# A new order for the operations of a fused gated-delta-rule and softplus-FFN kernel, from the 88th operation on

## The chip, the cores and the metric

The kernel runs on one NeuronCore of a Trainium2 chip. The metric is the device time of one execution in microseconds (us), input and output in the chip's main memory. Five engines work side by side, each through its own list in order: PE (matrix products), DVE and ACT (vector and activation work), POOL (vector work, and issue of some transfers) and SP (issue of transfers). They wait for one another by semaphores.

## The reference, cut to what matters

For each of 4 batches and 8 heads a 48 x 48 state is carried over 768 positions; the result goes through a feed-forward layer.

```python
k_n = k / (norm(k, axis=-1) + 1e-6)
for t in range(768):
    readout = q[t] @ state
    y[t] = g[t] * readout
    v_old = state.T @ k_n[t]
    state = state + beta[t] * outer(k_n[t], v[t] - v_old)
x = y as (3072 tokens, 384)
out = softplus(x @ w_in) @ w_out          # 384 -> 2048 -> 384
```

Inputs and output are float32; the kernel computes products in float16 with float32 accumulation.

## The kernel before, in words

The 768 positions are cut into 12 chunks of 64. Within a chunk the recurrence is turned into matrix products, for which each chunk needs the inverse of a 64 x 64 triangular matrix per head; only the state passes from chunk to chunk. Chunks 2i and 2i+1 share one inverse, so there are six inverses, named here by their first chunk (0, 2, 4, 6, 8, 10).

The function `load` (and `load_q`, for q) moves a chunk's k, q, v, g in two halves each, nearly all by SP; buffers are few (kf 3, qf 2, vf 3, gf 3), so a load often waits until an operation on DVE, ACT or POOL has freed one. The weights w_in (w0.0 to w0.3) and w_out (w1.0 to w1.3) are eight transfers that POOL issues.

The steps of a chunk pair, with the names used below:

- norms (`norms`): `ksq` (ACT, square, line 545), `red` (DVE, sum, 549), then the square root: `sqrt` on ACT for chunks 0 to 3, `pow` on POOL (566) for the others, and `eps` (DVE, 570 and 572). `kmul` (327) multiplies k by the result.
- products of k and q (`front`): `cast` of q to float16, transposes `trs` (345 for k, 388 for q), their copies `kev`, the products `gram` (503, and 432 and 461 for the first pair), from which `kkc` copies and `mask` (518) multiplies.
- the inverse (`inverse`): `kd0`, `kd1` (604) and `ln` (611) lay out the diagonal blocks; `clear` (619), `diag` (621) and `prep` (629) set up; 15 `step`s (639 and 646) eliminate, row by row, each needing the one before. For pair 0 this is on DVE, for all others on POOL. `cv` (228) and `c16` turn the result to float16, `tn` (667) and `t32` (686) transpose it on DVE, and PE completes the inverse by `xmm` (707), `tmm` (732) and `zmm` (770), with `xs`, `tlo`, `thi`, `z` between them.
- the chain from chunk to chunk (`chain`): `vs` and `w0` (first pair), `ks` and `qs` (813), `w` (847), `umm` (855), `u1`, `zu` (878), `u2`, `smm` (898), `s` (the new state, 913), `ymm` (928), `y` (943), `ytr` (962), `xt`.
- the feed-forward layer (`dense`): 96 groups `g1` (992), each followed by `soft` on ACT (1004), and 96 groups `g2` (1019), then a copy `o` and two stores per 128 tokens. `h`, into which g1 writes, has two buffers.
- 24 `warm` groups on PE (1064) that multiply the identity and whose result nobody reads.

Each step is an operation with a number (0 to 1255). What sets the order is a table written out in the program, `_ORDER` (line 1074 on): each word is an engine's letter (P = PE, D = DVE, A = ACT, G = POOL, S = SP) and an operation's number. `emit` goes through it, asserts that all that an operation depends on has been emitted, gives it its buffers in the order of the table, and puts its instructions at the end of that engine's list. So the table sets each engine's order, the engine of those operations that several engines can do, and which operation gets which buffer. Nothing is reordered later.

Of the kernel before, what the change touches and what calls it, by code (L numbers as in the profile page):

```python
# [1071 lines left out]


_ORDER = """
S0 D158 P1232 P1234 P1233 P1235 A1 P1236 P1238 D111 P1237 P1239 P114 A9 A104 D105 A110 P112 S8
A106 D115 P1241 D113 P124 P121 A123 D134 P137 A138 D133 P135 P1243 D125 P147 D107 D122 A136 P144
A108 P1240 P127 P1242 A149 P1249 A148 A146 D126 P1248 D109 D156 S19 S18 A145 S2 P1250 A206 P207
S3 A116 A117 A208 P118 A120 S5 S17 A119 P150 A152 S12 A129 S33 A154 D159 S27 S26 D157 D160 D161
D162 D163 D164 D165 D166 D167 D168 D169 D170 D171 P128 S16 D172 D173 D174 P1251 D175 D176 D177
P1244 A197 S25 D198 A222 P223 A224 G179 S11 A140 D178 G238 G239 P1245 A131 P1246 P1247 S24 A199  # L1080
P181 D180 S10 A139 P184 A182 D200 S4 D588 D132 D130 G188 A185 G187 P183 A190 P193 D194 A189 A594
P595 S13 A589 S32 P590 A201 D202 D203 D219 P186 A596 A591 P597 A598 P592 P605 A593 P603 S7 S6
D606 D604 A191 P204 P609 P607 A587 S34 D192 A275 D205 P209 D608 P214 S35 S42 S43 D211 A610 D210
D216 P220 G96 A212 A217 A215 D213 P141 A221 A142 A143 D218 D276 S41 S40 A277 P600 P599 D601 D602
P195 G300 D196 P872 D278 G99 A873 P230 A231 P225 A228 P1255 A226 A233 A235 D232 D229 D227 D611
D234 P874 A875 P886 D236 P619 P612 D620 D613 P151 D155 A284 P884 G98 A887 A885 G97 S14 D237 P285
P1254 A286 P882 P301 A883 A302 P615 A616 S49 P622 A623 P876 S15 A877 P878 G100 G101 G103 P614
P617 G279 D280 P621 P624 D153 S48 A879 A625 A618 G102 D281 P282 D297 P1252 D283 P630 D631 P632
D633 P292 A293 P298 A299 P880 A881 P634 A295 G240 G241 D294 D635 G242 G243 G244 G245 G246 P1253
G247 G248 P303 A304 G249 G250 G251 G252 G253 D306 D307 S50 P308 D296 A309 A311 P904 A905 P916  # L1090
A917 D312 P287 A290 D288 A313 P914 G254 G255 G256 D305 A915 P888 P910 A911 D314 D315 P627 P626
D629 D628 A353 D257 D258 P912 A913 P908 D354 P889 G259 D260 A909 G316 G317 P906 A907 G318 G319
G320 P902 A903 P890 P891 S57 A892 S56 P261 A262 G321 A267 P264 D265 A355 P895 P896 D291 P638
P266 P263 A270 D289 P643 P636 D310 G322 P897 P898 A268 P271 D356 G357 S20 S21 D644 A269 A899
P646 A647 D637 P639 A640 P918 S51 D362 P363 D272 A364 P641 A642 P645 P648 A649 S59 S58 A378 D358
P919 P920 P921 A922 D359 P650 P651 D653 P654 D652 S22 S23 D655 P656 P273 P925 P379 D657 A380
D274 P660 P667 P658 G323 G324 G325 G326 G327 A659 P926 P669 S28 S29 D668 G375 P670 A671 S65 S64
A431 D661 P663 D664 P927 D432 P672 A673 P662 P665 A666 S31 P360 D361 P376 S30 P678 D679 A377
P680 D681 P365 A366 D367 A368 D369 P928 P682 D683 P381 D383 A384 G328 G329 G330 G331 G332 G333
P386 A389 D388 D387 P956 S72 S73 A433 D385 A957 D434 P962 P370 D371 D390 D372 A963 A373 A382  # L1100
P954 A955 P936 A937 A391 P675 S74 P674 P934 G334 A935 G335 D336 S66 D374 S67 G440 G337 D676 S894
S36 D338 D677 D392 P944 S901 A945 S923 P342 A343 D393 P339 P952 A953 S37 S44 A340 A346 P948 A949
P441 P940 A941 A345 P684 P691 D692 D685 A442 P341 P693 P344 D348 G435 D436 A347 D453 P942 A943
S75 P932 A933 P349 P687 P694 S81 S80 P686 G394 S45 D350 A509 G395 G396 G397 G456 G398 P960 G399
S924 S39 A695 A961 A929 P950 D688 P689 D690 P454 S38 A951 P946 A947 P938 S88 A939 P457 G400 A458
G401 G402 G403 G404 G405 D510 P958 A959 S89 P964 G406 G407 S893 S931 S91 P702 D703 S930 S90 P351
S54 P696 D697 D352 A511 D512 P965 P966 P967 D968 S970 G408 G409 G410 P698 A455 P459 A462 D461
D463 P699 D460 D700 P971 P972 D701 P973 P974 P464 D437 S900 P704 A975 S85 S969 P708 A465 P438
D468 A467 D466 D709 D705 P978 P715 D716 P711 A439 A712 P979 P448 D450 D452 D451 D449 P718 S47
S46 S60 G534 G411 S53 G412 A415 A719 D416 P710 P713 A714 P980 P981 P443 D445 D447 P717 P720 A982  # L1110
S52 A444 P726 D727 P985 A721 P706 A446 A469 P728 A424 D729 P722 P723 P535 A536 P730 D707 P986
P987 D731 P1000 S55 G513 A1001 P1014 A1015 D470 S83 D471 A423 P988 A989 P1008 P1010 G413 A1009
D414 P420 A1011 P417 A418 D724 D514 D725 D531 P1018 A1019 P994 A995 A421 P532 D533 D515 P998
A999 P739 P732 D733 S82 A518 P734 P419 P422 D740 G472 G473 G474 G475 D426 P1004 A1005 D425 P996
A997 P429 P427 P742 D430 A743 P735 A736 P1002 D428 A1003 P519 P741 P744 P737 G476 A745 P1020
A1021 D738 S991 S70 D520 G477 S983 P516 P1006 P750 D751 S977 A517 A1007 S69 S976 P542 D544 D545
A543 D546 P752 P992 S71 A993 D753 P1016 A1017 P521 D523 A522 D525 P746 A524 P747 S990 D748 D749
P1022 A1023 P1012 G478 G479 G480 A1013 G481 P526 D530 A527 A529 P537 A540 D539 D538 P763 D541
P1024 P1025 P754 S984 P1026 P1027 D528 P756 P758 S84 A755 S61 D764 P766 S87 A1028 G482 G483 G484
G485 G486 G487 G488 G489 G490 G491 D492 P495 S63 P498 S62 D757 S1030 A767 A499 A496 G547 P759  # L1120
D548 D549 P1031 P1032 P1033 P1034 A1035 S1037 P765 D760 G493 D494 A501 A502 P768 D769 P761 D762
P1038 P1039 P776 D777 P771 P774 P497 P500 S76 A503 P770 D775 P778 D779 P1040 P1041 A1042 P1070
A1071 P1062 A1063 P1045 P1072 A1073 S68 S1036 P1058 A1059 P1046 P1054 A1055 P1074 D772 D773 P780
D781 P787 P1047 A1075 P1048 A1049 P1064 A1065 S77 S1043 P1060 A1061 P783 A784 D788 P790 A791
G550 G551 G552 G553 G554 G555 G556 G557 G558 G559 G560 G561 G562 G563 G564 D504 P505 P1056 S78
A1057 P1080 A1081 P782 D506 P785 D786 G565 G566 G567 G568 G569 G571 P789 P792 D793 P1052 A1053
P1066 A1067 P798 D799 P794 P795 D796 P1078 A1079 D797 P1082 P804 D805 A1083 P813 P811 D812 S79
P507 P807 D572 D508 A580 D570 S1050 S1044 S93 D808 P800 D801 S1029 P814 D815 P1068 A1069 P1076
A1077 P1084 P1085 P1086 P1087 D1088 P816 A817 P806 P809 D810 S95 P576 P573 A574 S1051 P824 D825
P802 A803 S1089 P1091 P1092 P1093 P1094 P818 P822 D823 A577 P578 A1095 S1097 P575 A581 P819 D582  # L1130
D820 P826 A827 S1090 P1098 P1099 P1100 P1101 A1102 S86 S94 S1103 P1132 A1133 P1114 A1115 P1105
P1126 A1127 D821 P828 P837 D829 P835 P583 P1138 A1139 P1116 A1117 P1106 P1107 P1120 A1121 P1108
A1109 S1111 S92 P1140 A1141 D836 D584 D579 P838 A839 P831 A832 P1134 A1135 P1128 A1129 P840 A841
P830 P833 P1112 A1113 S1104 S1110 P848 D834 P846 P843 P842 P1118 A1119 P1130 A1131 D844 D845
P852 P859 P1122 D847 A1123 D849 P850 D851 D860 D853 P1124 A1125 P1142 A1143 P1144 P1136 P1145
P1146 A1137 P1184 A1185 P1147 D1148 S1149 S1150 P1178 P862 D863 P855 D856 P585 D586 A1179 P1158
P1159 P1160 P1161 A1162 P854 P857 A858 P861 P864 P1151 P1152 P1153 P1154 D1155 S1156 S1157 P1172
D865 P1174 P1165 P1166 A1173 A1175 P1167 P1168 D1169 S1170 S1096 P1182 A1183 P1176 A1177 P868
D869 P866 D867 P1186 A1187 P1180 A1181 P870 S1171 P1188 P1189 D871 P1204 A1205 P1208 A1209 P1190
P1191 A1192 S1194 P1206 A1207 S1193 P1212 A1213 P1195 P1196 P1202 P1210 A1203 A1211 P1197 P1198  # L1140
D1199 S1200 S1201 P1216 A1217 P1214 S1163 P1218 P1219 P1220 A1215 P1221 A1222 S1223 S1164 S1224
P1225 P1226 P1227 P1228 A1229 S1231 S1230
"""

# [1 line left out]
_INS = ['q', 'k', 'v', 'beta', 'g', 'moe_w_in', 'moe_w_out']  # L1146
_OUTS = [((3072, 384), 'float32')]


# [23 lines left out]
```

## Time and profile before

| | |
|---|---|
| median of 3 runs | 257.73 us (255.1 to 258.18) |
| the profiled execution, its own time | 255.46 us |
| its span, first to last instruction | 253.6 us |
| PE busy | 236.9 us (93%), 5040 matmuls |
| DVE, ACT, POOL busy | 153.7, 153.0, 127.1 us |
| moved by DMA | 27.56 MB |

Times in the profile count from the start of the span. "Busy" is the time in which an engine had an instruction in execution; matmuls overlap, so a busy PE need not be at its peak. "L707" is line 707 of the program. In a timeline a row gives start, duration, engine, line, operation, what is written and read, the number of instructions, and in brackets how long the engine had been idle before it and who ended that. PEclk is the clock that was granted to PE, in tenths of full speed.

### The profile page before, as it was taken

What the parts mean: (1) busy time and instruction counts of PE and PEld (TensorE: products, weight loads), DVE (VectorE), ACT (ScalarE), POOL (GpSimd) and SP (SyncE); (2) the same over time, 40 slices, a digit from 0 to 9 for tenths busy, and PEclk for the clock granted to TensorE, in tenths of its full rate; (3) what the DMA queues carried; (4) which work ended last, traced back from release to release, by engine and by line L of the source; (5) the groups of instructions that cost most, each with busy time, mean ns of one, the idle gap of its engine ahead of it and who ended that gap; (6) DMA issues with size and microseconds to landing.
All of it is one profiled execution on the core that took longest, in us unless ns stands there. A gap on an engine that the chain in (4) does not pass through costs nothing.

```text
span 253.6 us, 11355 instructions
## 1 busy us (share of the span) xinstructions
PE 236.9 (93%) x5040; PEld 160.5 (63%) x5040; DVE 153.7 (61%) x311; ACT 153.0 (60%) x285; POOL 127.1 (50%) x227
## 2 busy tenths in 40 slices
PE   7976588998989999999999999999999999999993
PEld 3543577676766765666766767755676565777751
DVE  7789888775893699759697588523843315313000
ACT  3557777686866579973777675456453475223530
POOL 8201653978879889988948859884000000000000
PEclk9999757799999999999999999999999999999999
DMA  8999999999990789083943850643024130112113
GB/s 111 198 181 178 178 179 180 186 195 176 176 153 6 173 180 157 4 200 83 156 98 84 170 99 22 124 83 80 3 66 93 23 80 0 34 32 48 34 47 78
DMA packets 86192, 27.56 MB, mean 109 GB/s; under 512 B 76288, under 2 KB 86144, under 8 KB 86144
## 3 DMA queue, kind: packets, MB, share of 16 engines
q1 hardware_dynamic: 80096, 23.21, 50.2%
q0 software_dynamic: 3968, 3.25, 8.2%
q10 hardware_dynamic: 2080, 0.39, 1.2%
q8 instruction: 39, 0.64, 1.2%
q14 instruction: 9, 0.07, 0.1%
HBM read 25.26 MB, written 4.72 MB: 118 GB/s over the span
## 4 chain that ended last, share of the span: by engine, by line
PE 76%; DVE 9%; DMA 4%; issue 3%; SPq 2%; ACT 2%; POOL 2%; ACTq 0%; DVEq 0%; POOLq 0%
PE h L992 25%; PE o L1019 23%; PE d L813 4%; DMA beta_l<-in_beta_dram 3%; PE d L855 3%; PE d L732 3%; PE d L770 3%; PE d L878 2%; PE d L928 2%; PE d L503 2%; PE d L707 2%; PE d L898 2%; PE d L388 2%; PE d L345 2%; POOL beta_l L175 2%
## 5 line engine op out<-in xcount | busy, mean ns | idle before, releaser
L1004 ACT ACTIVATE ga<-h 128x512 f16<-128x512 f32 x96 | 56.3, 598 | 33.4 <-PE h L992 27.6
L992 PE MATMUL h<-xt,w_in 128*128 128x512 f16 (+1 forms) x384 | 73.3, 330 | 0.1
L1019 PE MATMUL o<-w_out,ga 128*128 128x384 f16 x384 | 70.3, 326 | 1.4 <-issue 0.7
L1019 PEld LDWEIGHTS <-ga 128*128 128x128 f16 x384 | 35.7, 98 | 23.9 <-issue 1.8
L992 PEld LDWEIGHTS <-w_in 128*128 128x128 f16 x384 | 35.6, 99 | 20.7 <-issue 0.6
L639 POOL TENSOR_TENSOR tmp<-nn,tt 128x30 f32<-128x30 f32 (+7 forms) x75 | 30.1, 401 | 5.6
L646 POOL TENSOR_TENSOR tt<-tt,tmp 128x30 f32<-128x30 f32 (+7 forms) x75 | 29.4, 392 | 5.9
L566 POOL TENSOR_TENSOR nv<-nv,half_c 128x32 f32<-128x32 f32 x4 | 21.8, 5456 | 5.1 <-DVE nv L549 5.1
L218 ACT ACTIVATE kqt<-d 128x1024 f16<-128x1024 f16 (+1 forms) x21 | 18.4, 903 | 7.0 <-PE d L388 6.1
L218 ACT ACTIVATE osb<-o 128x384 f32<-128x384 f32 x18 | 8.8, 489 | 21.5 <-PE o L1019 21.4
L943 DVE TENSOR_TENSOR yg<-d,gf 128x384 f16<-128x384 f32 x24 | 12.8, 553 | 13.6 <-PE d L928 10.2
L1064 PE MATMUL o<-ident 128*128 128x512 f16 x72 | 19.3, 411 | 1.4 <-POOL ident masks.py:199 1.4
L847 DVE TENSOR_TENSOR w<-vf,d 128x384 f16<-128x384 f32 x22 | 11.3, 549 | 12.0 <-PE d L813 10.8
L218 ACT ACTIVATE u<-d 128x384 f16<-128x384 f32 x31 | 14.3, 491 | 7.1 <-PE d L878 3.3
L218 ACT ACTIVATE kk<-d 128x256 f16<-128x256 f32 (+1 forms) x34 | 12.8, 413 | 7.8 <-PE d L503 6.4
L518 DVE TENSOR_TENSOR mt<-d,mask 128x256 f16<-128x256 f32 x40 | 15.5, 418 | 3.2 <-PE d L503 1.9
L220 DVE CAST u<-d 128x384 f16<-128x384 f32 x17 | 9.1, 549 | 13.1 <-PE d L878 11.6
L813 PEld LDWEIGHTS <-kqt 48*64 48x64 f16 x704 | 13.3, 108 | 5.5 <-issue 5.3
L220 DVE COPY osb<-o 128x384 f32<-128x384 f32 x6 | 3.3, 556 | 21.6 <-PE o L1019 21.6
L813 PE MATMUL d<-s,kqt 48*64 48x48 f16 x704 | 16.4, 188 | 0.0
L545 ACT ACTIVATE ksq<-kf 128x768 f32<-128x768 f32 x12 | 10.1, 843 | 7.6 <-DMA kf<-in_k_dram 6.7
L220 POOL CAST tw<-tt 128x256 f16<-128x256 f32 x10 | 5.4, 563 | 16.1 <-DVE tt L646 16.0
(110 smaller groups left out, 380.1 us busy)
## 6 DMA issues: line engine op xcount, KB each, us to landing
qf<-in_q_dram SPq DMA_DIRECT2D x24, 192.0 KB, 5.1
vf<-in_v_dram SPq DMA_DIRECT2D x24, 192.0 KB, 5.2
gf<-in_g_dram SPq DMA_DIRECT2D x24, 192.0 KB, 4.2
out_dram<-osb SPq DMA_DIRECT2D x48, 96.0 KB, 2.4
kf<-in_k_dram SPq DMA_DIRECT2D x22, 192.0 KB, 5.1
w_in<-in_moe_w_in_dram POOLq DMA_DIRECT2D x4, 384.0 KB, 7.5
w_out<-in_moe_w_out_dram POOLq DMA_DIRECT2D x4, 384.0 KB, 12.9
kf<-in_k_dram ACTq DMA_DIRECT2D x2, 192.0 KB, 7.5
```

The source lines that it names most:

```text
L218: nc.scalar.activation(o, x, AF.Copy, scale=float(sign))
L220: ENG[en].tensor_copy(o, x)
L518: nc.vector.tensor_tensor(mt[c][m].ap[:, NP * p : NP * p + NP], gb[m].ap.rearrange("p (n b) -> p n b", n=NP)[:, :, C:], mask[:, None, :].b ...
L566: lambda en: nc.gpsimd.tensor_tensor(nv.ap, nv.ap, half_c, ALU.pow),
L639: eng.tensor_tensor(t, nn.ap[:, :, j + 1 :, j : j + 1].broadcast_to([P, 2, n, w]), tt.ap[:, :, j : j + 1, :w].broadcast_to([P, 2, n, w]), ...
L646: eng.tensor_tensor(rows, rows, t, ALU.add)
L813: nc.tensor.matmul(hd(o.ap)[HALF[r], NP * p + i], kq_of(c)[FEAT[m], 8 * p + 2 * i + r, off : off + C], s0[r].ap[FEAT[m], NP * p + i], **st ...
L943: lambda en, m=m: nc.vector.tensor_tensor(heads(yg.ap, m), hd(yp[m].ap), heads(gf.ap, m), ALU.mult),
L992: nc.tensor.matmul(hp.ap[:, n * b : n * b + n], w_in[:, j, f * P : (f + 1) * P], xt.ap[:, j, t0 : t0 + n], start=(j == 0), stop=(j == 2),)
L1004: lambda en, hp=hp, o=gb: nc.scalar.activation(o.ap, hp.ap, AF.Softplus),
L1019: nc.tensor.matmul(op.ap[:, :DM], b.ap[:, col + c0 : col + c0 + 128], w_out[:, f, :], start=(f == 0), stop=(f == NF - 1),)
L1064: nc.tensor.matmul(wb.ap.rearrange("p (a b) -> p a b", a=4), ident, ident[:, None, :].broadcast_to([P, 4, P]),)
```

## The change

Only the table `_ORDER` changes. It is described as an order searched anew behind an unchanged beginning of 87 operations, with a model in which a later weight transfer also shares with loads that still wait. All 1256 operations are in both tables, with the same shapes and dependencies. Engine by engine, the unchanged beginning shows as 30 operations of PE, 33 of DVE, 20 of ACT and 15 of SP; where words of the beginning stand differently in the two tables, each engine's own order there is the same. The instructions differ only where another engine does an operation: 17 more operations on DVE (278 for 261), 16 fewer on ACT (256 for 272), one fewer on POOL (123 for 124).

What is spoken of below, by its number: red 5 is 278, pow 4, 6, 8 and 10 are 279, 357, 435 and 513, ln 2 is 237, clear 2 and diag 2 are 238 and 239, prep 2.0 is 240, the steps of pair 2 are 242 to 256, cv 2 is 257 and c16 2 is 259, tn 2 is 258, xmm 2 and 3 are 261 and 264; clear 4 to prep 4.0 are 316 to 318, cv 4 is 335, tn 4 is 336, xmm 4 and 5 are 339 and 342; c16 0 is 179, cast q5.0 is 300, cast q7.0 is 378, u2 1.1 is 625, soft 0.14 is 887, eps 6 is 358, kmul k6 and k7 are 359 and 375, u1 3.1 is 671, zu 3.1 is 672, the transposes of k6 and k7 are 360 and 376; the weight transfers are 96 to 103, the loads of q7 are 58 and 59.

- On PE, the xmm of pairs 2, 4, 6 and 10 stand nearer to the beginning, that of pair 8 a little later.
- On POOL, c16 0 and clear 2 leave; the weight transfers but the first stand behind diag 2, which needs clear 2 (now on DVE); pow 6 and kmul k7 leave the midst of pair 4's steps and stand, with kmul k6 (from DVE), behind cv 4; cv 2 joins from DVE. kmul k9 and k11 join from DVE as well.
- On ACT, c16 0 stands ahead of ksq 2, and cast q7.0 ahead of u2 1.1 and soft 0.14.
- On SP, g0 and v0 come earlier, and q4 later, behind k5 and g1.

```diff
 _ORDER = """
...
-P181 D180 S10 A139 P184 A182 D200 S4 D588 D132 D130 G188 A185 G187 P183 A190 P193 D194 A189 A594
-P595 S13 A589 S32 P590 A201 D202 D203 D219 P186 A596 A591 P597 A598 P592 P605 A593 P603 S7 S6
...
-P195 G300 D196 P872 D278 G99 A873 P230 A231 P225 A228 P1255 A226 A233 A235 D232 D229 D227 D611
-D234 P874 A875 P886 D236 P619 P612 D620 D613 P151 D155 A284 P884 G98 A887 A885 G97 S14 D237 P285
-P1254 A286 P882 P301 A883 A302 P615 A616 S49 P622 A623 P876 S15 A877 P878 G100 G101 G103 P614
-P617 G279 D280 P621 P624 D153 S48 A879 A625 A618 G102 D281 P282 D297 P1252 D283 P630 D631 P632
-D633 P292 A293 P298 A299 P880 A881 P634 A295 G240 G241 D294 D635 G242 G243 G244 G245 G246 P1253
...
-P266 P263 A270 D289 P643 P636 D310 G322 P897 P898 A268 P271 D356 G357 S20 S21 D644 A269 A899
-P646 A647 D637 P639 A640 P918 S51 D362 P363 D272 A364 P641 A642 P645 P648 A649 S59 S58 A378 D358
...
-D274 P660 P667 P658 G323 G324 G325 G326 G327 A659 P926 P669 S28 S29 D668 G375 P670 A671 S65 S64
-A431 D661 P663 D664 P927 D432 P672 A673 P662 P665 A666 S31 P360 D361 P376 S30 P678 D679 A377
...
-S36 D338 D677 D392 P944 S901 A945 S923 P342 A343 D393 P339 P952 A953 S37 S44 A340 A346 P948 A949
...
+S27 P1249 D159 D157 A117 P1248 D160 P1250 D161 S26 P207 D162 D163 S16 D164 P118 S25 A208 D165
+P150 S11 D166 A120 A119 D167 A152 P128 D168 D169 D170 D171 A154 A129 D172 S7 D173 S4 S24 S10
+P1251 A131 S32 D174 D175 D176 D177 D178 A179 P1244 D180 G188 P1246 P1247 A197 D198 D132 A222
+D588 D594 P1245 S43 P181 A182 A187 P184 A185 P183 A190 S42 D589 P193 A189 P595 P590 D130 A199 S6
+G96 D200 D596 P1254 S13 P223 A201 D202 A591 D194 D203 P597 P1252 P592 A275 D276 A224 A139 D219
...
+A143 D608 D238 G239 P220 A221 S34 P204 P599 D205 P600 D602 P214 P230 D216 D215 D601 A587 A233
+A231 G97 G99 D232 D218 D234 G100 G98 P225 D229 G102 D228 A226 P619 D300 D227 A277 D278 A217 P209
+A210 D611 D211 G101 A212 S58 A235 S59 P301 D213 D620 A302 P195 D196 S56 S21 P621 P622 A284 D236
+A623 D237 P614 A378 S20 P612 P624 D613 G279 D280 D297 D281 S57 G103 A625 P886 A887 G240 G241
...
+P880 G257 D314 D315 P916 G316 A917 A881 P626 D258 P888 P912 P902 P889 G317 D312 G318 P627 G319
+G320 G321 G322 G323 G324 G325 G326 G327 G328 G329 G330 G331 G332 G333 G334 G335 D260 A267 A913
...
+P646 S75 A647 A353 P904 A905 S23 P645 D272 P648 D649 P641 S39 S44 D354 G357 P379 A380 P898 P656
+D642 P650 P651 D653 D652 P273 A899 S901 S28 P654 D655 A337 P660 D657 P658 D336 D274 S74 A659 S45
+D661 P667 D668 S65 P339 A340 D338 P342 D358 G359 P663 A362 A664 S83 A431 S31 P670 D671 G375 P662
+S73 P363 A364 P906 S72 D343 P669 P672 P665 A666 D456 S36 S46 D394 P360 P918 S80 A673 P376 G395
...
```

## The prediction

> **What bounds the kernel now.** I read the page's slices first, then the waits of PE, then the stretches between the places where PE waits for an inverse, and last POOL's and DVE's timelines, since POOL makes the inverses.
>
> ```profile
> PE   7976588998989999999999999999999999999993
> ...
> PEclk9999757799999999999999999999999999999999
> ```
>
> PE is short of work, and at a low clock, only in slices 3 to 8 (up to about 50 us). After that it is the bound. The stretches say it in microseconds (columns: stretch, its length, then busy time of PE, PEld, DVE, ACT, POOL, clock, DMA share, GB/s):
>
> ```profile
> 25.25:44.20 18.95, 14.46 (x411) 12.91 (x411) 16.07 (x29) 14.23 (x30) 10.03 (x12) 0.64 1.06 179
> 44.20:51.86 7.66, 7.16 (x112) 4.83 (x112) 6.12 (x12) 5.39 (x9) 6.25 (x3) 0.78 1.26 185
> 70.54:97.93 27.39, 26.59 (x750) 18.58 (x749) 21.11 (x41) 19.60 (x36) 24.05 (x40) 1.00 0.74 131
> 97.93:253.60 155.67, 150.76 (x3103) 100.35 (x3102) 76.11 (x134) 85.67 (x159) 62.72 (x117) 1.00 0.37 74
> ```
>
> The boundaries 70.54 and 97.93 are the starts of xmm of chunks 2/3 and 4/5, the first PE work that needs an inverse made on POOL. PE executes its list in order, so an xmm that stands too early in it stops everything behind it. Today both stand just right:
>
> ```profile
> 70.54 1.19 PE L707 MATMUL d<-tn,kk 64*64 64x32 f16 x64 [0.20 <-DVE tn L667]
> ...
> 97.93 1.19 PE L707 MATMUL d<-tn,kk 64*64 64x32 f16 x64
> ```
>
> 0.20 us of waiting at the first, none at the second. Behind the second inverse lie 155.67 us, of which PE works 150.76. So the end is set by when that xmm starts, plus the PE work behind it. What makes the inverse (POOL, then DVE):
>
> ```profile
> 44.29 5.46 POOL L566 TENSOR_TENSOR nv<-nv,half_c 128x32 f32<-128x32 f32 x1 [4.02 <-DVE nv L549]
> 49.73 0.82 POOL L297 DMA_DIRECT2D w_out<-in_moe_w_out_dram  x1
> 51.86 1.20 POOL L629 TENSOR_TENSOR nn<-ln,beta_l 128x256 f32<-128x256 f16 x2 [1.32 <-DVE nv L570]
> ...
> 68.34 0.91 POOL L220 CAST tw<-tt 128x256 f16<-128x256 f32 x2
> 69.52 0.52 POOL L619 MEMSET tt<- 128x512 f32 x1 [0.27 <-DVE tv L228]
> 70.11 0.24 POOL L621 COPY tt<-beta_l 128x32 f32<-128x32 f32 x1
> 70.28 1.19 POOL L629 TENSOR_TENSOR nn<-ln,beta_l 128x256 f32<-128x256 f16 x2
> ...
> 85.70 1.48 POOL L327 TENSOR_TENSOR kn<-kf,nv 128x768 f16<-128x768 f32 x1
> ...
> 93.22 1.86 POOL L228 TENSOR_SCALAR tv<-tt,own 128x256 f16<-128x256 f32 x2
> ```
>
> POOL waits for DVE's red 5 (L549), does pow 4 (5.46) and a weight issue, and starts the inverse of chunks 2/3 (prep) at 51.86; the next inverse follows at 70.28, broken by pow 6 and kmul k7.
>
> **The change, part by part.** No instruction is added or removed but by the engine that runs it (two clears and 13 kkc move to DVE, three kmul to POOL, and so on). Everything is about the order.
>
> *PE's list.* xmm 4/5 now stand before 15 dense groups (7 g1, 8 g2), 4 gram, 3 transposes, ytr and two each of qs, smm, umm, zu, ymm, which stood ahead of them. By the chain's rows (g1 0.66, g2 0.65, gram 0.28, transposes 0.50, the small ones 0.25 to 0.31, ytr 0.4) that is 9.8+1.1+1.5+0.4+2.8 = 15.6 us. What is left from xmm 4 to the end becomes 155.7+15.6 = 171.3. So xmm 4 must start by 97.9-15.6 = 82.3 for the time to stay as it is. xmm 2/3 stand before four g1 more (2.6 us).
>
> *When prep 2.0 starts.* It still stands behind red 5, pow 4 and one weight issue. Between cv 0 (ends 25.33) and red 5, DVE now has 33 operations where it had 26: both w0, u1 0.1, kev q1.0, clear 2, cast q5.0 and the masks of chunk 3 come ahead of it. By their rows they take 18.4 us end to end, so red 5 ends at 43.7 at the earliest (44.20 today, where the same stretch held about 16 us of work and 3 of waiting). Followed by hand, it waits for ksq 3 (on ACT behind c16 0, xs and thi), for ymm 0.0 and for trs k2.0 (PE takes k3 first), 3.9 us together, and ends at 47.6. Then pow 5.46 and the weight issue 0.82: prep 2.0 at 53.9 (floor 50.0; today 51.86). ln 2 follows red 5 on DVE (vs, two masks, w, z, kd1, ln: 5 us), so it does not decide.
>
> *From prep 2.0 to xmm 4.* prep and 15 steps took 16.4 us in the first POOL chain (51.86 to 68.28) and 14.4 in the last (156.67 to 171.04); I take 15.4 each. c16 2 (0.91) and now also cv 2 on POOL (1.86; on DVE today, 1.09) stand between, with clear and diag: 3.7 with gaps. Then 15.4 again, now without pow 6 and kmul inside, cv 4 and tn 4 3.0. Sum 37.5, so xmm 4 starts at 91.4 (floor 50.0+35.5 = 85.5).
>
> *Is PE there by then?* PE would come to xmm 2 earlier than its inverse (73.3) and wait, unless ACT holds it first: cast q7.0 now stands on ACT ahead of u2 1.1 and soft 0.14, and q7's loads are issued only after cast q5.0 (about 46) and beside six weight transfers, which wait for clear 2 on DVE and start at about 40. In the trace such neighbours cost much: from 40 to 55 us the weights' queue moved 132 to 147 GB/s and the loads' 36 to 58, and a load issued at 37.08 landed at 52.42. So q7 lands at about 58, PE stands at its third g1 from about 53 to 60, and reaches xmm 4 at 88 to 91. POOL's chain and this path end together; I keep 91.4.
>
> *Behind xmm 4.* pow 6, kmul k6 and kmul k7 moved behind cv 4, and DVE's eps 6 (with u1 3.1 behind it) with them: kmul k6 ends 5.5+0.7+1.5-1.1 = 6.6 us after xmm 4 starts, and PE needs it after 3.8 us of work (zu 3.1 needs u1 3.1 little sooner): 2.8 us, and 0.2 for k7. The later inverses have room: at the same pace that of chunks 6/7 ends at about 127, PE comes to it at 135.
>
> *The clock.* Granted clock was halved from 28.0 to 41.65 and from 45.07 to 48.48, where PE had idled 1.83 and 1.34 us at a time; the shortest low stretch is 3.41 us. I add one behind the wait for kmul k6: half of 3.41, 1.7 us. [...]
>
> *Sum.* 91.4+171.3+3.0+1.7 = 267.4 of span; the profiled execution lies 255.46-253.6 = 1.9 above its span: 269.3 on its basis. That execution is near the lowest of the three runs (median 257.73). Since the 15.6 us that moved are work without waits, which can fill some of the 5 us that PE idles behind 97.93, I take 1.3 off: **268 us**.
>
> **Rivals.**
> 1. *Almost no change.* DVE waits for nothing (prep 2.0 at 50.0), the steps run at the last chain's pace (xmm 4 at 85.5), and the moved work covers the wait for kmul: 85.5+171.3+1.9 = 259, down to 257. For it: DVE had only 2.9 us of idle between 25.25 and 44.20 today. Against: red 5 then needs every producer in time, and the slots of q, k and d hang together. It decides once xmm 4 is below 88; a gain of 2% would need it at 77, below every floor here.
> 2. *ACT's wait for q7 is longer.* If loads beside weights move at the 5.3 us each of the before trace from the first on, q7.1 lands at 63, kd0 4 and ln 4 come at 78, the second chain starts 5 us later: 273 to 276. For it: the same six transfers made those landings, one of 19.5 us. Against: the loads' queue is empty for some us before q7, so the weights get ahead.
> 3. *The early part is faster than I follow it.* Weights issued late leave the DMA to k4, k5, g0 and q4, PE gets its two fillers there and keeps the clock, and all of it starts some 10 us sooner: under 252. Against: pow 4 behind red 5 keeps prep 2.0 at 50 or later.
>
> **How the numbers follow.** Forecast (262.9 to 272) 0.60; rival 1 0.17; rival 2 0.16; rival 3 0.07. The range takes most of rivals 1 and 2: 258 to 276. Measurement can tell 2% from no change: 252.6 to 262.9 is "within". Faster 0.06, within 0.16, slower 0.78.
>
> **What would show it.** In the changed profile: prep 2.0 (L629 on POOL) at 52 to 55; xmm 4 (third pair on L707) at 90 to 94 with PE idle before it or before xmm 2, by DVE tn (L667); ACT idle before a cast of q (L218) for qf by several us between 50 and 60; PE waiting about 3 us for a kmul (L327) soon after xmm 4; PEclk below 9 beside these waits. It is wrong if xmm 4 starts before 86, or if PE idles long after 140, where I have it full.

## The result, and the profile after

The changed kernel takes 266.86 us (median of 4 runs, 266.2 to 267.93) against 257.14 us before (4 runs, 255.1 to 258.18): a ratio of 1.039, with a 95% interval of 1.032 to 1.047. The forecast was 268 us, slower. The profiled execution of after took 266.2 us, 264.5 of it span.

The page's slices of after (tenths of PE's busy share, tenths of the granted clock, 6.6 us each) show where: the gaps that before had only up to 50 us now go on to almost 100 us, and the clock is low a second time (from 90.08 to 96.91 us). Behind that PE is full, as before.

```profile
PE   7975897989789789999999999999999999999993
PEclk9999586599999869999999999999999999999999
```

One place lets the two executions be compared: the transposes of k7 on PE. They start at 89.63 us in before and at 98.89 in after, and what is left behind them is nearly the same. Stretches of after (length, busy time of PE, PEld, DVE, ACT, POOL, clock, DMA share, GB/s): from xmm 2 to the transposes of k7, from xmm 4 to them, and from them to the end.

```profile
73.17:98.89 25.72, 22.06 (x651) 17.85 (x651) 17.11 (x30) 15.85 (x28) 22.54 (x39) 0.87 0.62 109
...
90.09:98.89 8.80, 8.06 (x187) 6.83 (x187) 5.97 (x11) 4.80 (x9) 8.06 (x5) 0.61 0.80 131
...
98.89:264.50 165.61, 160.67 (x3227) 105.95 (x3225) 85.15 (x155) 86.80 (x157) 68.61 (x119) 1.00 0.40 74
```

The same two stretches of before, from xmm 2 to the transposes of k7 and from them to the end:

```profile
70.54:89.63 19.09, 18.34 (x587) 13.92 (x587) 13.13 (x23) 12.65 (x22) 16.48 (x26) 1.00 0.65 111
...
89.63:253.60 163.97, 159.00 (x3269) 105.01 (x3266) 84.09 (x151) 92.61 (x173) 70.29 (x131) 1.00 0.40 79
```

So of the 10.9 us of span, 2.6 are there when xmm 2 starts (73.17 for 70.54), 6.6 come between xmm 2 and the transposes of k7 (25.7 us for 19.1), and 1.6 are work left behind them (165.6 for 164.0). In the middle stretch PE has about the same work: after has six g2 fewer there, and four g1 and xmm 4 and 5 more, which by the rows of before makes 18.3 us in both (an estimate; before was busy for 18.34). Before does it in 19.1 us, with 0.75 us of idling; after needs 25.7, with 0.87 of the clock and 3.7 us of idling.

PE's timeline of after shows the places (start, duration, line, operation, what is written and read, number, and the idle time before it with who ended it):

```profile
73.17 0.68 PE L707 MATMUL d<-tn,kk 64*64 64x32 f16 x32 [1.89 <-DVE mt L518]
74.49 0.62 PE L707 MATMUL d<-tn,kk 64*64 64x32 f16 x29 [0.64 <-DVE s L913]
...
90.09 1.89 PE L707 MATMUL d<-tn,kk 64*64 64x32 f16 x64 [0.95 <-DVE tn L667]
...
97.42 0.43 PE L878 MATMUL d<-u,z 64*64 64x48 f16 x16 [0.67 <-ACT kqt L218]
97.78 0.62 PE L345 MATMUL d<-ident,kn 128*128 128x128 f16 x8
...
98.89 0.61 PE L345 MATMUL d<-ident,kn 128*128 128x128 f16 x8
```

PE stands 1.9 us before xmm 2, 0.6 before xmm 3, 0.95 before xmm 4. Behind xmm 4 it stands only once, 0.67 us before zu 3.0, but it runs with half the clock (0.50 from 90.08 to 96.91 us): xmm 4 and 5 take 1.89 us for 64 products where before, at 1.00, took 1.19. The wait of zu 3.0 is for kev q6.0 on ACT (kqt, L218), and ACT's timeline says what that copy stood behind:

```profile
95.61 0.84 ACT L545 ACTIVATE ksq<-kf 128x768 f32<-128x768 f32 x1 [2.40 <-DMA kf<-in_k_dram]
96.36 1.01 ACT L218 ACTIVATE kqt<-d 128x1024 f16<-128x1024 f16 x1
```

It is ksq 8, which waited 2.40 us for a load of k8. From zu 3.0 on PE does not stand again up to the transposes of k7.

POOL's timeline of after shows what the inverses and the two kmul waited in line for:

```profile
45.39 6.11 POOL L566 TENSOR_TENSOR nv<-nv,half_c 128x32 f32<-128x32 f32 x1 [0.98 <-DVE nv L549]
...
52.30 2.56 POOL L629 TENSOR_TENSOR nn<-ln,beta_l 128x256 f32<-128x256 f16 x2
...
69.94 1.85 POOL L228 TENSOR_SCALAR tv<-tt,own 128x256 f16<-128x256 f32 x2
...
72.61 1.20 POOL L629 TENSOR_TENSOR nn<-ln,beta_l 128x256 f32<-128x256 f16 x2
...
87.13 1.84 POOL L228 TENSOR_SCALAR tv<-tt,own 128x256 f16<-128x256 f32 x2
88.93 5.47 POOL L566 TENSOR_TENSOR nv<-nv,half_c 128x32 f32<-128x32 f32 x1
95.13 3.22 POOL L327 TENSOR_TENSOR kn<-kf,nv 128x768 f16<-128x768 f32 x2 [0.74 <-PE d L388]
```

POOL goes from prep 2.0 (52.30) through the inverse of pair 2, cv 2, the inverse of pair 4, cv 4 and pow 6 to both kmul, which end at 96.61 and 98.36, with one pause of 0.74 us ahead of them (in it DVE does eps 6, which needs pow 6). The transposes of k6 start 1.2 us behind the first, those of k7 0.5 us behind the second. In before kmul k7 ended at 87.18. What was bought with that is the inverse of pair 4, ready at 90.04 (end of tn 4) in place of 96.99; but tmm 4, the next step that uses it on PE, starts at 102.91 in after and at 101.86 in before, and chunk 4's ks at 112.6 against 101.5. That the inverse was early gained nothing for its next reader.

### The profile page after: what moved, and what is told of

It reads as the page before. It is cut to its first block, busy times and chain, and to the rows that moved or that the text cites. A ratio compares the mean times of both kernels' runs of the same rounds, so it can differ in the third digit from the quotient of the medians.

```text
span 264.5 us, 11331 instructions
## 1 busy us (share of the span) xinstructions
PE 243.5 (92%) x5040; PEld 164.8 (62%) x5040; DVE 160.0 (61%) x327; ACT 145.6 (55%) x265; POOL 131.0 (50%) x225
## 4 chain that ended last, share of the span: by engine, by line
PE 67%; POOL 11%; DVE 7%; DMA 6%; ACT 4%; issue 2%; SPq 1%; ACTq 0%; DVEq 0%; POOLq 0%
PE o L1019 22%; PE h L992 21%; PE d L813 3%; DMA beta_l<-in_beta_dram 3%; POOL tt L646 3%; PE d L878 2%; PE d L855 2%; POOL nv L566 2%; DMA kf<-in_k_dram 2%; PE d L928 2%; POOL tmp L639 2%; PE d L770 2%; PE d L732 2%; PE d L707 2%; POOL beta_l L175 2%
## 5 line engine op out<-in xcount | busy, mean ns | idle before, releaser
L992 PE MATMUL h<-xt,w_in 128*128 128x512 f16 (+1 forms) x384 | 75.1, 333 | 1.3 <-ACT ga L1004 1.2
L639 POOL TENSOR_TENSOR tmp<-nn,tt 128x30 f32<-128x30 f32 (+7 forms) x75 | 27.3, 363 | 5.9
L220 DVE CAST u<-d 128x384 f16<-128x384 f32 x22 | 11.9, 550 | 18.3 <-PE d L878 11.3
L1064 PE MATMUL o<-ident 128*128 128x512 f16 x72 | 20.2, 427 | 1.4 <-POOL ident masks.py:199 1.4
L813 PE MATMUL d<-s,kqt 48*64 48x48 f16 x704 | 19.1, 193 | 0.9 <-DVE s L913 0.4
L813 PEld LDWEIGHTS <-kqt 48*64 48x64 f16 x704 | 15.8, 113 | 5.4 <-issue 5.2
L218 ACT ACTIVATE u<-d 128x384 f16<-128x384 f32 x26 | 12.4, 488 | 11.9 <-PE d L855 8.8
L218 ACT ACTIVATE kqt<-d 128x1024 f16<-128x1024 f16 (+1 forms) x18 | 15.8, 903 | 5.0 <-PE d L388 4.5
L218 ACT ACTIVATE osb<-o 128x384 f32<-128x384 f32 x17 | 8.3, 489 | 15.8 <-PE o L1019 15.7
L518 DVE TENSOR_TENSOR mt<-d,mask 128x256 f16<-128x256 f32 x40 | 15.6, 417 | 1.5 <-PE d L503 0.9
L707 PE MATMUL d<-tn,kk 64*64 64x32 f16 x384 | 9.0, 190 | 6.2 <-DVE tn L667 3.7
L228 POOL TENSOR_SCALAR to<-td,own 128x512 f16<-128x512 f16 x3 | 5.0, 1671 | 18.3 <-DVE td L686 18.3
```

Of the source, the lines that this page charges most:

```text
L218: nc.scalar.activation(o, x, AF.Copy, scale=float(sign))
L220: ENG[en].tensor_copy(o, x)
L518: nc.vector.tensor_tensor(mt[c][m].ap[:, NP * p : NP * p + NP], gb[m].ap.rearrange("p (n b) -> p n b", n=NP)[:, :, C:], mask[:, None, :].b ...
L639: eng.tensor_tensor(t, nn.ap[:, :, j + 1 :, j : j + 1].broadcast_to([P, 2, n, w]), tt.ap[:, :, j : j + 1, :w].broadcast_to([P, 2, n, w]), ...
L707: nc.tensor.matmul(xp.ap[HALF[r], HC * u : HC * u + HC], kk.ap[HALF[r], 16 * cl + u], tn.ap[HALF[r], 16 * cl + u].rearrange("p x j -> p (x ...
L813: nc.tensor.matmul(hd(o.ap)[HALF[r], NP * p + i], kq_of(c)[FEAT[m], 8 * p + 2 * i + r, off : off + C], s0[r].ap[FEAT[m], NP * p + i], **st ...
```

## The experiments

All ratios are to the kernel before, timed beside it on the same chip. Numbers of operations are those of the table; all but the warm groups that three runs add or move do the work of both kernels.

### Where the loss arises: the two tables joined

```diff
 h1: _ORDER = before's words for operations that start before 70.4 us in its profile
+             + after's words for all others
 h2: _ORDER = after's words for operations that start before 68 us in its profile
+             + before's words for all others
 h3: as h2, cut at 50 us
```

> The 365 operations that start before 70.4 us in the profile of before, in the order of before; all the others in the order of after. xmm 2 then starts at about 70.5 as before, and from there the order of after runs: its xmm 4 follows 16.9 us behind xmm 2 in the profile of after, so 87.5 to 88, and 174.4 us lie behind it there, less 2.6 for four g1 groups that are already done: 260.0 of span, some 261 to 262 as a time. Theory of the prediction (PE waits at xmm 2 and xmm 4 for POOL's inverses and for kmul behind them; the loss lies behind xmm 2): 260 to 264, a ratio to before of 1.012 to 1.028. Rival (the loss lies in the first 70 us, by the late q7, the low clock and the later inverse of pair 2): 259 or less, ratio 1.007 or less.

> The mirror image: the 336 operations that start before 68 us in the profile of after, in its order, the others in the order of before (so pow 6 and kmul k7 stand in the midst of pair 4's steps again, and xmm 4 behind the dense work). PE has lost 3.2 us more than in the profile of before by 70 us (idle and low clock together), and xmm 2 starts at about 71.5 in place of 70.5. Theory: that loss is kept, since PE is full from there on, and no more than it: 258.5 to 261, ratio 1.006 to 1.016. Rival (the early part is the cause): 264 or more, ratio 1.027 or more.

> As the run before, but only the 242 operations that start before 50 us in the profile of after stand in its order. It leaves out cast q7.0 ahead of u2 1.1 and soft 0.14, and prep 2.0 at 52.3 stays. If the step with q7 costs what PE lost behind 50 us (at most 2 us), this run is 1 to 2 us faster than the one that keeps the order to 68: 257 to 259. If the early loss comes from the weights behind clear 2 and the low clock from 42.3 to 52.5 alone, both runs are equal within 0.7 us.

Measured: h1 263.93 us against 255.95, ratio 1.033 (1.029 to 1.038); h2 263.99, 1.030 (1.023 to 1.037); h3 258.94, 1.013 (1.007 to 1.018). A stretch of h1:

```profile
70.00:100.00 30.00, 26.41 (x696) 20.75 (x695) 19.87 (x35) 16.58 (x28) 25.06 (x42) 0.72 0.69 120
```

and of h3:

```profile
70.00:100.00 30.00, 29.66 (x777) 21.04 (x775) 23.90 (x46) 21.32 (x39) 24.75 (x44) 1.00 0.72 127
```

With before's beginning, the later part of after costs 8.0 us, inside the range of the theory, and the rival (259 or less) is out: from 70 to 100 us PE idles 3.6 us and has 0.72 of the clock, and from xmm 2 to the transposes of k7 it takes 25.9 us (25.7 in after). With after's beginning to 50 us and the rest of before, the same 30 us are full (29.66) at full clock, and the kernel is 3.0 us slower: xmm 2 starts at 73.68, 3.1 later than in before, and that delay stays to the end. The two parts together, 11.0, are as much as the whole loss (9.7 by the medians, 10.9 by the two profiles' spans).

h2 missed its number and came out where its rival had put it (264). But PE waits 3.5 us for `soft` between 69 and 75 us, because before's list puts dense groups ahead of xmm 2 whose forerunners the other beginning had not done; xmm 2 starts at 79.0. The seam itself costs there, so h2 says less than h3. h3's time lies in the range that was to speak for the step with q7 (257 to 259), but that range was meant against an h2 without the seam. h3 leaves out the step with q7 and loses its 3 us all the same, with as much time lost between 40 and 60 us as after. In it the inverse of pair 2 ends on POOL at 69.66, and DVE takes 1.9 us more for ln 4 and two s before its cv 2. How much of the 3 us each early move costs was not separated further.

### What an early place of xmm costs

```diff
 (PE's list of before)
-P370 P954 P936 P675 P674 P934 P944 P342 P339
+P370 P339 P342 P954 P936 P675 P674 P934 P944
```

> The kernel before with one thing moved: xmm 4 and 5 on PE stand ahead of four g1 groups (2.11, 2.2, 2.1, 2.6) and both smm 3, work of 3.1 us by the rows. The inverse isn't made sooner (tn 4 ends at 97.0 in the profile of before). Theory of the prediction (all that is moved behind an xmm whose inverse is not ready is lost, because PE is full behind it): PE waits 2.2 to 3.1 us at xmm, 259.0 to 260.5, ratio 1.008 to 1.013. Rival (the moved work fills the 5 us that PE still idles behind 97.93): within 0.7 us of before.

Measured: 259.44 us against 255.95, ratio 1.015 (1.011 to 1.019), so 3.5 us for 3.1 us of work moved. The time is inside the theory's range, the ratio a little above it (1.008 to 1.013). PE's timeline shows the wait:

```profile
96.69 1.28 PE L707 MATMUL d<-tn,kk 64*64 64x32 f16 x64 [2.34 <-DVE tn L667]
```

and the stretches ahead of and behind it what the wait brings with it:

```profile
94.20:97.61 3.41, 1.07 (x70) 0.92 (x60) 2.69 (x6) 1.03 (x3) 3.41 (x5) 1.00 1.20 177
97.61:101.02 3.41, 3.41 (x48) 1.44 (x44) 0.00 (x0) 0.93 (x2) 3.41 (x1) 0.50 0.81 144
```

PE waits 2.34 us, and then has half the clock for 3.41 us, in which it does dense work: 1.7 us more. So this wait of 2.34 us costs about 4 (2.34 and 1.7), of which a little is made up later.

### Filling the waits with useful work

If what costs is that PE has nothing in its list at these places, dense groups from behind should fill them.

```diff
 s1, PE's list of after
-P660 P658 P667 P339 P342 ... P906 ... P360 P918 P376
+P660 P906 P658 P667 P918 P339 P342 ... P360 P376
 s3, s1 and
-D358 D671 ... A664 ...           P665 P360
+D671 D358 ... A664 A909 A907 ... P665 P919 P920 P921 P360
 s5, after, and
+P914 P908 P895 P261 P264 ... P906 P660 P918 P919 P658 P667 P920 P921 P339 P342
+... P665 P925 P926 P927 P360 P376
+A913 A903 A892 A267 ... A909 A337 A907 ... A664 A922; D671 D358
 s9, as s5, but
-P925 P926 P927 ahead of P360, A922 behind A664
+A364 ahead of A431
```

> The changed kernel (after) with two dense groups on PE, g1 1.4 and g2 1.0.0 (1.3 us), moved from behind xmm 4 into the 1.9 us that PE idles just ahead of it in the profile of after. xmm 4 itself stays at about 90.1, since POOL makes its inverse no sooner. With that work PE should keep the full clock where it was halved from 90.1 to 96.9. Theory A (the wait for kmul and for u1 3.1 behind eps 6, which pow 6 makes late, ends at 95 to 98 whatever the clock is, so the clock's 1.7 us and the wait's 3.0 us of the prediction are not two terms but one): PE gains only the one group that stood behind that wait, 0.6 to 1.3 us, 265.6 to 266.3. Theory B (the two add up, as the prediction had it): 1.3 us of work and the 3.4 us lost to the clock, 262 to 263.

> The run before it, and three steps more so that PE has work while kmul k6 and k7 are late: u1 3.1 on DVE ahead of eps 6, soft 1.6 and 1.4 on ACT right behind u1 3.0, and g2 1.0.4, 1.0.8 and 1.0.12 on PE ahead of the transposes of k6. If the wait for kmul (3.0 us in the prediction) is real and hidden under the low clock in the profile of after, four groups (2.6 us) now lie in it: 2.5 to 3.5 us faster than after, 263.3 to 264.4. If PE loses nothing there, the groups only change places: 266 to 267.

> All waits of after between 70 and 98 us filled with dense groups: ahead of xmm 2 three (g1 1.12, g1 1.6, g2 0.1.0; with soft 1.10, soft 1.0 and o 0.0 on ACT ahead of tlo 2.0), ahead of xmm 4 five (g1 1.4, g2 1.0.0 to 1.0.12; with soft 1.6 and 1.4 on ACT around c16 4), ahead of the transposes of k6 three (g2 1.1.0 to 1.1.8; with o 1.0 on ACT behind u1 3.0). POOL's order, and with it the start of both inverses, stays that of after. Theory of the prediction (what costs time is that PE's list leaves it without work at these places, since dense work stands behind them): 11 groups of 0.65 us less what was done in these places before, 5 to 7 us faster than after, 260 to 262. Rival (POOL's later inverse and late pow 6 cost it by themselves, whatever PE does meanwhile): less than 3 us faster, 264 or more.

> As the run with all waits of after filled, but g2 1.1.0 to 1.1.8 and o 1.0 stay where after has them, behind the transposes of k6 and k7, and the copy kev q6.0 on ACT stands ahead of ksq 8. In that run the transposes of k6 came 3.1 us later than in after, and with them kev k6, red 8 and y 3 on DVE (5 us of idle there), and zu 3.0 waited 1.2 us for kev q6.0, which stood behind ksq 8. If these two are what took its gain back, 1.5 to 2.5 us faster than after: 264.4 to 265.4. If the low clock from 77 to 87 us (10 us of it in that run, where the chain of small products runs alone behind xmm 2) took it back, no better than that run: 266 to 267.5.

Measured: s1 267.53 us, ratio 1.045 (1.041 to 1.050); s3 269.78, 1.054 (1.048 to 1.061); s5 266.61, 1.041 (1.035 to 1.047); s9 269.82, 1.050 (1.043 to 1.057). After itself has 1.039 (1.032 to 1.047). None is faster than after, and s3 is slower clear of the intervals. Of the numbers that these runs were to show only that of s5's rival came (264 or more: what POOL does late costs by itself, whatever PE does meanwhile); all others were missed.

Why, by their traces: in s1 the stretch at half clock is not gone, it lies from 95.0 to 101.9 in place of 90.1 to 96.9, where dense groups stand; the transposes of k7 come 0.6 us sooner and that is lost again before 110. Just ahead of them PE waits for kmul k7 on POOL, which ends at 98.28:

```profile
98.33 1.03 PE L345 MATMUL d<-ident,kn 128*128 128x128 f16 x8 [0.54 <-POOL kn L327]
```

In s5 PE no longer waits at xmm 2, and what it has done by the transposes of k7 is 3.9 us more than in after, but they start at 101.34, 2.4 us later. PE's waits of s5 between 90 and 106 us:

```profile
PE d L962 <- DVE yg L943: 1.3, 1, 1.3
PE d L878 <- ACT kqt L218: 1.2, 1, 1.2
```

The first is ytr 3: DVE held y 3 behind the copy of k6, which waits for the transposes that had been moved back. The second is zu 3.0 behind kev q6.0, which stands behind ksq 8 on ACT. Both had been named for s9, which takes the first cause away and puts kev q6.0 ahead of ksq 8; its two waits are down to 0.6 and 0.5 us, and it gained nothing: its transposes of k7 start at 98.78, 0.06 us after kmul k7 ends, and behind 45 us, 28 us of it run at half clock (14.4 in after, 18.4 in s5). Which of the two costs how much there was not separated. So in s5 the dense groups put into a wait on PE's list pushed back the chain on that list (the transposes of k7 by 2.4 us in s5), and the chain held up the lists of DVE and ACT; and where the chain then ran alone, from 77 to 87 us, the granted clock was 0.5.

### Holding the clock

Eight warm groups more in the late part of after (s6), eight more in its early part (s7), twelve more in the first chain of before (b2), and three of before's own moved (w1).

```diff
 s6, after: IDLE = 32, P906 ahead of P658, and
+P1256 P1257 P339 P342 P1258 P663 ... P1259 P363 ... P1260 P669 P1261 P672 P1262 P665 P1263 P360
 s7, after: four + eight groups in the last set of warm
+P1256 P214; P1257 P225; P1258 P619; P1259 P209; P1260 P301; P1261 P621; P1262 P624; P1263 P874
 b2, before: four + twelve
+P1256 P1257 P181; P1258 P183; P1259 P193; P1260 P590; P1261 P186; P1262 P605
+P1263 P609; P1264 P209; P1265 P141; P1266 P1267 P225
 w1, before
+P1253 P181; P1254 P1252 P225; P895 P896 P261 P264; P952 P948 P342 P339
```

> The changed kernel (after) with the full clock held from 87 to 98 us and nothing else gained: g1 1.4 stands ahead of ytr 2.0 again, and eight warm groups more (results that nobody reads, 0.65 us each at full clock) stand ahead of xmm 4 (two), umm 3.0, the transpose of q6, qs 3.1, zu 3.1, zu 3.0 and the transposes of k6 (one each), where PE waited or ran at half clock. Runs so far: from 68 to 106 us PE of after loses 5.6 us idle and 3.2 us by the low clock, and filling the place ahead of xmm 4 alone only pushed the low stretch behind it. If the low clock is a cost of its own, 2.5 to 3.5 us faster than after: 263.5 to 264.5. If the end of this stretch is set by pow 6, kmul and what follows on DVE and ACT, the clock there costs nothing: 265.5 to 268.

> The same in the early part of after: eight warm groups more between 39 and 54 us, ahead of gram 2.1, gram 3.0, ks 1.1, gram 2.0, the transpose of q5, qs 1.1, zu 1.1 and g1 0.2, where the clock was halved from 42.3 to 52.5. If xmm 2 waits for POOL in any case (prep 2.0 at 52.3, PE idle 1.9 us before xmm 2), PE's gain there turns into a longer wait at xmm 2: 266 to 267.5, xmm 2 at 72.5 to 73.5. If the low clock is what costs the early 3 us: 263 to 265.

> The kernel before with twelve warm groups more between 25 and 45 us (ahead of xmm 0 two, tmm 0, zmm 0, umm 0.0, tmm 1, ymm 0.1, ytr 0.1, gram 2.0, the transpose of q1 one each, gram 3.0 two), where its clock is halved from 28.0 to 41.7 and PE idles 4.6 us. They keep the array above 2800 columns in each 3.41 us. If the low clock sets how fast the first chain goes, red 5 and with it pow 4 and prep 2.0 come earlier, and the whole kernel follows: 1.5 to 3 us faster than before, ratio 0.988 to 0.994. If the chain is set by DVE and ACT there, or the groups delay it: same to 2 us slower, ratio 0.998 to 1.008.

> The kernel before with three warm groups, which stand in the full part of PE's list (at 50.8, 56.2 and 60.1 us, 0.65 us each), moved into waits: two ahead of gram 3.0, one ahead of xmm 0. So that xmm 2 and xmm 4 don't take the gain back as waits, both are moved behind two dense groups more (g2 0.1.0 and 0.1.4; g1 2.10 and 2.8). If PE is full from 46 us on and its clock falls when a stretch of 3.41 us holds too little array work (as it seems from the profiles so far: below about 2800 columns of the full array), two warm groups (3072 columns) keep the clock at full behind gram 3.0 and 1.9 us of useless work leave the full part: 1.5 to 3 us faster than before, ratio 0.988 to 0.994. If the waits for inverses and chain set the end all the same: within 0.7 us.

Measured: s6 268.91 us, ratio 1.048 (1.041 to 1.056); s7 267.07, 1.042 (1.035 to 1.049); b2 259.85, 1.013 (1.005 to 1.020); w1 260.08, 1.017 (1.011 to 1.022). One stretch of s6:

```profile
87.00:98.90 11.90, 11.48 (x277) 7.39 (x272) 8.24 (x15) 5.05 (x9) 11.04 (x7) 1.00 0.88 143
```

and the same of after:

```profile
87.00:98.90 11.90, 9.37 (x225) 7.83 (x225) 8.29 (x15) 6.46 (x12) 11.07 (x8) 0.71 0.72 124
```

s6 has the full clock there, and from xmm 4 to the transposes of k7 it takes 8.9 us as after does (8.8), with six warm groups done in between. Its time lies above both theories' ranges, and s6 as a whole gained nothing. POOL's work is the same (11.04, 11.07), and kmul k7 ends at 97.91. That sets a floor: with the full clock and without the extra groups the transposes of k7 could start at about 98, which is 0.9 us sooner than in after at most (an estimate; the extra groups themselves keep PE too busy to show it). In s1 PE waited at this floor (kmul k7 ends at 98.28 there), and in s9 the transposes of k7 started 0.06 us behind it. In after they started 0.5 us behind it, since zu 3.0, which stands ahead of them, had waited for kev q6.0 on ACT. s7 shows the same for the early part. Its PE has the full clock where after has half:

```profile
42.29:52.53 10.24, 9.74 (x228) 6.11 (x228) 9.26 (x19) 5.53 (x10) 9.26 (x5) 1.00 1.21 210
```

and xmm 2 stands as in after, behind a wait of 1.88 us:

```profile
73.42 0.79 PE L707 MATMUL d<-tn,kk 64*64 64x32 f16 x28 [1.88 <-DVE mt L518]
```

as the first theory had it. b2 holds the full clock up to 77 us where before had 0.64 of it:

```profile
25.25:44.20 18.95, 17.73 (x439) 11.49 (x437) 15.49 (x27) 14.10 (x30) 10.06 (x12) 1.00 1.05 181
```

and yet red 5 ends at 44.55 (44.20 in before) and xmm 2 starts at 70.73 (70.54). So holding the clock by such groups gains nothing there. That the low clock by itself costs nothing is not shown: z 0 on DVE ends 6.7 us behind cv 0 in b2 and 7.1 in before, but y 0, which needs a product that has warm groups ahead of it on PE, starts 10.9 us behind it and 10.5 in before. Between xmm 2 and xmm 4 b2 loses 3.5 us: PE stands 1.7 us in the midst of tmm 2, for nothing that the profile shows, and then runs at half clock from 77.23 to 80.64. Why it stands there stays open.

w1 missed its sign. The warm groups that seemed useless in the full part had, it seems, been keeping the clock: without the one at about 56 us it is halved from 56.5 to 63.4, over dense groups (the 3.41 us before that held 1951 columns, by the count of the last section; a warm group has 1536), and xmm 2, moved behind two more groups, comes at 74.1. The run changed both things, so their shares stay open.

## Why the prediction was right, and where it was not

1. *xmm 4's place* (15.6 us of work moved behind it, 171.3 us left): right. xmm 4 started at 90.09 for 91.4, and 174.4 us followed for 176.0. a1 confirms the price of such a move by itself (3.5 us for 3.1 moved). h1 fits the size: with before's beginning and xmm 4 at 88.64 the prediction's terms give 88.6 less 82.3 and the wait's 3.0, so 9.3 us, and it measured 8.0; but h1 holds all that changes behind 70 us.
2. *prep 2.0*: 52.30 for 53.9. The step erred in red 5, for which DVE was to wait 3.9 us; it ended at 45.31, not 47.6. cv 0 was done at 24.47, not 25.33, and DVE's waits from there came to 2.1 us. Part of that was lost again, since pow 4 took 6.11 us, not the 5.46 of its row before.
3. *prep 2.0 to xmm 4*: 37.8 us for 37.5, cv 2 and cv 4 on POOL at 1.85 and 1.84 as their row said.
4. *q7 holding ACT*: the wait is there, its size was wrong. ACT's timeline:

```profile
51.97 0.84 ACT L218 ACTIVATE qn<-qf 128x768 f16<-128x768 f32 x1 [3.46 <-DMA qf<-in_q_dram]
```

   q7 was issued at 44.14 and 44.72 and landed at 50.70 and 51.88, not 58: they took 6.6 and 7.2 us beside six weight transfers; the three loads after them whose landing is recorded took 11 to 17. PE stood 1.2 us, not 7. In h3 the early loss is as large without this step, though h3 has a delay of its own there (1.9 us on DVE).
5. *The wait for kmul* (3.0) *and the clock* (one stretch, 1.7): the time lost is about the wait's, and the clock was counted on top of it. kmul k6 ended 6.5 us after xmm 4 started, as the prediction had it (6.6). From xmm 4 to the transposes of k7 PE had 4.9 us of work at full speed and took 8.8, so 3.9 more. But no row of after shows PE waiting for a kmul: the clock was halved from 90.08 to 96.91, two stretches of 3.41 us and not one, and from xmm 4 on and not behind the wait. PE worked slowly through the time that it would otherwise have stood. So the two are one term: pow 6 and kmul on POOL set a floor, at which PE waits in s1, and the clock adds 0.9 us at most to it. That ACT holds kev q6.0 behind ksq 8 and its load, for which PE stood 0.67 us, the prediction did not have. In the sum, 171.3 and the wait's 3.0 make 174.3 where 174.4 followed xmm 4: the clock's 1.7 is what was too much.
6. *The moved work fills other waits* (1.3 off): not separated.
7. *Later inverses have room*: right, though less of it. tn 6 ended at 133.31, not 127, and xmm 6 took it at 134.64.

The sum was 267.4 of span, measured 264.5: 1.3 too late at xmm 4, 1.6 too much behind it. That the time came within 1.2 us is in part luck: the 1.3 taken off for filled waits, which no run shows, nearly cancels the clock's 1.7, and a slower pow 4 hid part of the error in red 5. Rival 1 needed xmm 4 below 88, rival 2 needed q7 at 63, rival 3 needed an early part 10 us sooner; none came.

What the prediction did not see is why the wait behind xmm 4 can't be bought back: it took PE's list for the thing to be filled. The traces put two lists in its place: POOL's, with pow 6 and both kmul behind the inverse of pair 4, and ACT's, with ksq 8 ahead of kev q6.0; and an xmm 4 that stands 12.8 us ahead of tmm 4. This is read from traces. No run took after and moved only pow 6 and the two kmul back on POOL, or only xmm 4 back on PE; what each of them costs alone is not shown.

## What to carry to other kernels

Before a matrix that one engine makes slowly is made earlier, look up when its first reader, and the reader's own next step, could run: here 7 us gained on the inverse did not bring its next reader forward, and the two multiplications that it overtook came 11 to 15 us later. A wait on an in-order list can't be filled freely, since what is put into it also stands ahead of the chain and of the lists that wait for that chain: s5 had 3.9 us more of PE's work done by the transposes of k7, and they came 2.4 us later. And the wait of a1 was paid for twice, by its own 2.34 us and by the 3.41 us of dense work behind it at half clock (1.7 us more).

## What the runs showed of the hardware that was not expected

In the first 160 us of the 14 profiles of this study the granted clock changed 90 times, and within a profile all changes lie whole multiples of 3.413 us apart (to 0.02 us), so on one grid. From profile to profile the grid lies elsewhere, and the same order of work had its slow stretches in other places: after and s1 have the same lists up to about 85 us, and the clock falls first at 25.23 us in the one and at 19.95 in the other, 5.28 us or 1.55 steps of the grid apart.

Neither the longest idle gap nor PE's busy time tells in these traces whether the clock falls. In after the longest gaps at its three falls were 2.76, 0.48 and 0.95 us, and at a gap of 1.89 us it did not fall. Three pairs of neighbours of after's grid (the clock is the third number from the end):

```profile
38.88:42.30 3.42, 2.16 (x81) 1.51 (x81) 2.91 (x8) 3.23 (x7) 2.92 (x5) 1.00 1.05 184
42.30:45.71 3.41, 2.74 (x50) 2.14 (x51) 3.41 (x9) 2.42 (x6) 2.43 (x4) 0.50 1.09 159
...
69.60:73.02 3.42, 1.69 (x24) 0.98 (x21) 1.20 (x2) 0.00 (x0) 3.30 (x6) 1.00 0.60 123
73.02:76.43 3.41, 2.62 (x89) 2.29 (x89) 3.41 (x7) 2.34 (x5) 2.86 (x9) 1.00 0.02 5
...
86.67:90.08 3.41, 1.55 (x51) 1.13 (x46) 2.63 (x6) 1.65 (x3) 3.23 (x5) 1.00 0.53 100
90.08:93.50 3.42, 3.34 (x113) 3.18 (x113) 2.48 (x4) 2.04 (x4) 3.42 (x1) 0.50 1.19 169
```

PE was busy 2.16 us in the first stretch and the clock fell; it was busy 1.69 us in the second, with a gap of 1.9 us that ran over its end, and the clock stayed. The second held full 128 x 128 tiles, the first mostly small ones. Count each product as its columns times its tile's share of the 128 x 128 array, as far as its time lies in the stretch: the first then held 1566 columns, the second 3221, the third 1148. There are 600 whole stretches in the 14 profiles up to 150 us, and the two bounds that follow are chosen to fit them. Of the stretches at full clock, those with less than 2250 columns were followed by half clock in 31 cases of 31, those with 2250 to 3100 in 14 of 25, those with more in none of 444. Of the stretches at half clock, those under 2250 were followed by half clock in 42 of 42, those between in 13 of 27, those above 3100 in none of 31. At full clock 12 products of 256 columns take 1.31 us in after (from 236.18 us), so about 8000 columns would fit into a stretch, and the two bounds are 28 and 39% of that (an estimate from these numbers). The count goes by the modelled ends of the matmuls, so the band between may partly be its own error. It tells which stretches were followed by half clock in these profiles; what sets the clock it does not show.

pow 4 took 6.11 us in after and 5.46 in before, with the same shape on the same engine, while weights and loads moved in both. No run here tells why.
